# Rows of cumulated logs made in place by TensorE for ten chunks, and four units' low words shifted by ScalarE

## The chip, the cores and the metric

The kernel runs on one core of a Trainium2 chip. The metric is the device time of one execution in microseconds (us). Five engines work side by side, each through its own queue in order: TensorE (PE, with its weight loads shown apart as PEld), VectorE (DVE), ScalarE (ACT), GpSimd (POOL) and SyncE (SP), which here only issues transfers.

## The reference

A state-space layer in chunks, then a two-matrix layer with an activation of its own. In the reference:

```python
log_a = np.log(np.clip(a, 1e-06, 1.0))
for c in range(nc):
    cum = np.cumsum(la, axis=-1)
    L = np.exp(cum[:, :, :, None] - cum[:, :, None, :]) * causal
    M = np.einsum('bhin,bhjn->bhij', Cc, Bc) * L
    y[:, :, sl] = M @ xc + (C @ state) * exp(cum)
    state = exp(sum(la)) * state + sum_j B x exp(cum_last - cum)
h = y_as_rows @ w_in          # 3072 x 256 by 256 x 2048
out = (h - np.tanh(h)) @ w_out
```

The batch is 4, there are 8 heads of dimension 32, the state has 16 entries, the sequence 768 steps. `moe_w_in` and `moe_w_out` arrive as 64-bit floats.

## The kernel before

**Tiling.** A sequence is cut into chunks of 112 steps (the last has 96); the 28 chunks of the four batches are numbered so that chunk `ck` is step block `ck // 4` of batch `ck % 4`. The first 16 of the 128 partitions carry the state, so that one matmul does the state's part and the chunk's own. The second layer works on column tiles of the 3072 tokens: four of 256 (`t` = 0 to 3), then four of 512. The first tile needs the outputs of chunks 0, 1 and 2; its hidden units are taken in eight "units" `u` of 256. In a first sweep the four small tiles use units 0 and 1 alone, later sweeps take the small tiles in pairs.

**Order.** Nothing is issued directly. Each step is announced with `op(engine, cost, function, reads, writes)` to a planner (`Order`, L64). It knows the dependences and a cost for each step, plans by a list schedule in several rounds with random jitter (from `SEED`), takes the best plan, and issues the functions in its order of start times. Tags such as `po0` or `ph` stand for places in PSUM or SBUF with a number of buffers; a new holder waits for the readers of the old one. `urge` moves a step ahead.

**Decay factors.** The exponent of chunk, head, i, j is `cum_i - cum_j`. The kernel has three ways:
- Chunks 0 to 3 (`first_tile`, L435): for each half of the heads POOL cuts the logs to a triangle (`fn_k`, L443), PE adds a mask of -32768 (`fn_f`, L448) and sums the triangle with four full f32 matmuls (L451), ACT takes the exp (`fn_x`, L467), PE makes the products of B and C (`fn_p`, L461), DVE multiplies (`fn_m`, L471). The mask is in the exponent, so nothing is cut afterwards.
- Chunks 4 to 9 (`chunk_a`, L494): the row sums are split by DVE into three bf16 parts (`split`, L1039), stored to memory (`put_parts`, L1050) and read back in eight small transfers (`get_parts`, L1053) into `lt_c` and `rt_c`, beside rows of ones (`ones`, L989) and signs (`signs`, L993). Four bf16 matmuls of nine rows (L507) then give the exponents next to the products (L512) in one PSUM tile `att`; ACT exp (L516), DVE product (L520), and POOL cuts the upper triangle (`cut`, L532).
- Chunks 10 on (`chunk_l`, L535): rows of sums are broadcast from memory (`cumr`), ACT subtracts through its bias (L550), POOL cuts.

`chunk_y` (L623) multiplies the factors with x (L637); its tag is `po0` for odd chunks under 4, else `po1`. `prep` (L378) fills the state's rows and the decayed B on POOL; `state` (L562) starts the running state.

**Weights.** `conv(u)` (L314) turns a unit's 64-bit words into f32 and then into a high and a low part: ACT scales the high words (`fn0`, L325), DVE shifts the low words by 29 (`fn1`, L330), clamps (L335) and puts the bits together (L338, L345), ACT rounds to the high part (L349), DVE subtracts (L352). Units 0 and 1 come in halves. The first tile multiplies units 0 and 1 in plain f32 (`plain`, L756), and the small tiles take their second matrix as f32 too (L834); all else uses three products of high and low parts (`mm1` L763, `mm2` L844), with tanh (L794), difference (L798), and the split of the result (L802, L808) between them.

Of the kernel before, what the change touches and what calls it, by code (L numbers as in the profile page):

```python
# [222 lines left out]
def tile_ssm_moe(ctx: ExitStack, tc: tile.TileContext, a, x, bn, bc, wts, out):  # L223
# [90 lines left out]
    def conv(u, halves=False):  # L314
# [12 lines left out]
        def fn1(s):  # L327
            if s.start == 0:
                wm[u] = p1.tile([P, 2, 512], U32, tag="wm", name=f"wm{u}")
            nc.vector.tensor_scalar(out=wm[u][:, s], in0=raws[u][:, s, :, 0], scalar1=29, scalar2=None,  # L330
                                    op0=ALU.logical_shift_right)
# [103 lines left out]
    def first_tile():  # L435


        n_a = op.pieces(slot("att", 1), 2)
        place = {}

        def fn_k(ck, i):
            chs[ck]["k", i] = p3.tile([P, BANK], F32, tag="g", name=f"lm{ck}_{i}").rearrange("p (h m) -> p h m", h=4)
            nc.gpsimd.affine_select(out=chs[ck]["k", i], in_=la[:, 4 * i : 4 * i + 4, ck : ck + 1].broadcast_to([P, 4, P]),  # L443
                                    pattern=[[0, 4], [-1, P]], compare_op=ALU.is_gt, fill=0.0, base=0, channel_multiplier=1)

        def fn_f(ck, i):
            f = chs[ck]["f", i] = ps_h.tile([P, 4, P], F32, tag="ph", name=f"cp{ck}_{i}")
            nc.tensor.matmul(out=f[:, :, 0:Q], lhsT=eye, rhs=never.unsqueeze(1).broadcast_to([P, 4, Q]),  # L448
                             start=True, stop=False, skip_group_check=True)
            for h in range(4):  # L450
                nc.tensor.matmul(out=f[:, h, 0:Q], lhsT=chs[ck]["k", i][:, h], rhs=upto[:, N:P], start=False, stop=h == 3,  # L451
                                 skip_group_check=True)

        def fn_p(ck):
            if ck == 0:
                att = ps_a.tile([P, 4, 4 * P], F32, tag="att", name="att0")
                place[0] = att[:, :, 0 : 4 * Q].rearrange("p i (k q) -> p i k q", k=4)
            bb, cc = operands(ck)
            for i in range(4):
                r = slice(32 * i, 32 * i + 2 * N)  # L460
                nc.tensor.matmul(out=place[0][:, i, 2 * (ck % 2) : 2 * (ck % 2) + 2], lhsT=bb[r], rhs=cc[r],  # L461
                                 start=True, stop=True)
# [11 lines left out]
        for ck in range(FIRST):
            urge = URGE if ck < len(chunks[0]) else 0.0
            k = chs[ck]
            k["n_l"] = op.pieces(slot("lt", NL), 2)
            if ck % CPG == 0:
                prep(ck // CPG)
            for i in range(2):  # L480
                n_f, n_k = slot("ph", NPH), slot("g", 3)
                op("POOL", 0.7, lambda ck=ck, i=i: fn_k(ck, i), r=["la"], w=[n_k], urge=urge)
                op("PE", 1.14, lambda ck=ck, i=i: fn_f(ck, i), r=[n_k, "upto", "never"], w=[n_f])
                op("ACT", 0.52, lambda ck=ck, i=i: fn_x(ck, i), r=[n_f, "tab"], w=[k["n_l"][i]], urge=urge)
                if i == 0:
                    op("PE", 0.59, lambda ck=ck: fn_p(ck), r=[grp[ck // CPG]["n_bc"]], w=[n_a[ck % 2]])
                op("DVE", 0.6, lambda ck=ck, i=i: fn_m(ck, i), r=[n_a[ck % 2]], w=[k["n_l"][i]], urge=urge)
            if ck == 0:
                for i in range(4):
                    for j in range(2):  # L490
                        op("SP", 0.7, lambda i=i, j=j: get_parts(i, j), r=["cum3"], w=[("lt_c", "rt_c")[j]], dma=KB // 2)
            chunk_y(ck)

    def chunk_a(ck):  # L494

        d, k, q = grp[ck // CPG], chs[ck], qlen(ck)
# [1 line left out]
        n_a = slot("att", 1)  # L500

        def fn_p():
# [7 lines left out]
            for i in range(4):  # L510
                r = slice(32 * i, 32 * i + 2 * N)
                nc.tensor.matmul(out=at_[:, i, 2:4, :], lhsT=bb[r], rhs=cc[r, :, 0:q], start=True, stop=True)  # L512
# [687 lines left out]
```

## Time and profile before

| what | us |
|---|---|
| median of three runs | 324.19 |
| lowest and highest | 323.92, 324.3 |
| the profiled execution's own time | 324.25 |
| its span, first to last instruction | 322.6 |
| PE busy in the span | 313.7 |
| DVE, ACT, POOL busy | 215.3, 210.3, 60.6 |

The profile is a record of one execution. Times of the timeline count from the start of the span. A line of a timeline has start, duration, engine, line of the kernel, operation, the written and read tiles, the shape and the number of instructions; in brackets stands how long the engine was idle before it and what it waited for. "SPq" rows are the issue of a transfer, not the transfer. Matmuls overlap: the distance between the starts of two says what one costs, the duration also holds its latency. An f32 matmul leaves two records.

### The profile page before, as it was taken

What the parts mean: (1) busy time and instruction counts of PE and PEld (TensorE: products, weight loads), DVE (VectorE), ACT (ScalarE), POOL (GpSimd) and SP (SyncE); (2) the same over time, 40 slices, a digit from 0 to 9 for tenths busy, and PEclk for the clock granted to TensorE, in tenths of its full rate; (3) what the DMA queues carried; (4) which work ended last, traced back from release to release, by engine and by line L of the source; (5) the groups of instructions that cost most, each with busy time, mean ns of one, the idle gap of its engine ahead of it and who ended that gap; (6) DMA issues with size and microseconds to landing.
All of it is one profiled execution on the core that took longest, in us unless ns stands there. A gap on an engine that the chain in (4) does not pass through costs nothing.

```text
span 322.6 us, 5757 instructions
## 1 busy us (share of the span) xinstructions
PE 313.7 (97%) x2160; PEld 255.3 (79%) x2160; DVE 215.3 (67%) x314; ACT 210.3 (65%) x471; POOL 60.6 (19%) x94
## 2 busy tenths in 40 slices
PE   8997999999999999999999999999999999999995
PEld 7765888788888878787878887888878788888883
DVE  6978997898888867457563864664765645645552
ACT  6568888477687888575945854966868544534451
POOL 8604424003122514402300400111102000000000
PEclk9999999999999999999999999999999999999999
DMA  6679557539433149280606005005420000100001
GB/s 205 195 238 325 173 162 307 183 94 346 89 65 66 30 98 272 48 241 5 205 0 207 16 0 209 1 2 226 168 61 0 2 0 0 68 1 0 2 0 65
DMA packets 15451, 35.27 MB, mean 109 GB/s; under 512 B 2464, under 2 KB 4416, under 8 KB 15424
## 3 DMA queue, kind: packets, MB, share of 16 engines
q1 hardware_dynamic: 13696, 31.76, 29.4%
q0 software_dynamic: 1728, 3.15, 5.7%
q8 instruction: 17, 0.28, 0.4%
q14 instruction: 10, 0.08, 0.1%
HBM read 28.32 MB, written 3.43 MB: 98 GB/s over the span
## 4 chain that ended last, share of the span: by engine, by line
PE 91%; DVE 5%; ACT 2%; issue 1%
PE ph L763 39%; PE o L844 38%; PE o L834 3%; PE y L704 3%; PE att L678 3%; PE y L637 1%; PE warm L1003 1%; DVE lt L471 1%; ACT lt L550 1%; DVE lt L520 1%; DVE wv L345 1%; PE att L461 1%; PE cp L451 1%; ACT lt L516 1%; DVE wm L338 1%
## 5 line engine op out<-in xcount | busy, mean ns | idle before, releaser
L798 DVE TENSOR_TENSOR g<-ph,g 128x512 f32<-128x512 f32 x96 | 65.7, 688 | 52.1 <-ACT g L794 52.0
L794 ACT ACTIVATE g<-ph 128x512 f32<-128x512 f32 x96 | 57.3, 598 | 48.7 <-PE ph L763 47.8
L808 DVE TENSOR_TENSOR gl<-g,gh 128x512 fp32r<-128x512 f32 x88 | 62.7, 715 | 31.0 <-ACT gh L802 29.5
L763 PE MATMUL ph<-xh,wh 128*128 128x512 f32 (+1 forms) x200 | 76.0, 382 | 0.0
L763 PE MATMUL ph<-xh,wl 128*128 128x512 f32 (+1 forms) x200 | 74.8, 377 | 0.0
L802 ACT CAST gh<-g 128x512 fp32r<-128x512 f32 x88 | 54.4, 620 | 28.3 <-DVE g L798 26.4
L844 PE MATMUL o<-gh,wh 128*128 128x512 f32 x176 | 69.2, 393 | 0.0
L844 PE MATMUL o<-gl,wh 128*128 128x512 f32 x176 | 68.5, 389 | 0.0
L844 PE MATMUL o<-gh,wl 128*128 128x512 f32 x176 | 68.5, 389 | 0.0
L763 PE MATMUL ph<-xl,wh 128*128 128x512 f32 (+1 forms) x200 | 59.0, 376 | 0.0
L532 POOL TENSOR_SCALAR_AFFINE_SELECT lt<-lt 128x896 f32<-128x896 f32 (+1 forms) x24 | 23.3, 969 | 128.4 <-ACT lt L550 118.3
L763 PEld LDWEIGHTS ph<-xh,wh 128*128 128x128 f32 x200 | 37.6, 188 | 7.6 <-issue 0.6
L763 PEld LDWEIGHTS ph<-xh,wl 128*128 128x128 f32 x200 | 37.6, 188 | 6.8
L763 PEld LDWEIGHTS ph<-xl,wh 128*128 128x128 f32 x200 | 36.7, 188 | 7.0
L550 ACT ACTIVATE lt<-lt,ncum 128x112 f32<-128x112 f32 (+1 forms) x144 | 41.7, 375 | 0.0
L844 PEld LDWEIGHTS o<-gh,wh 128*128 128x128 f32 x176 | 33.0, 188 | 7.8 <-issue 0.8
L844 PEld LDWEIGHTS o<-gl,wh 128*128 128x128 f32 x176 | 33.0, 188 | 6.9
L844 PEld LDWEIGHTS o<-gh,wl 128*128 128x128 f32 x176 | 33.1, 188 | 6.7
L684 DVE TENSOR_TENSOR lt<-att,lt 128x896 f32<-128x896 f32 (+1 forms) x18 | 18.9, 1052 | 0.0
L888 POOL DMA_DIRECT2D pt<-part x12 | 11.1, 1023 | 41.1 <-ACT part L885 38.1
L834 PE MATMUL o<-g,wf 128*128 128x256 f32 x64 | 15.4, 384 | 1.4 <-ACT x L578 0.9
L605 ACT CAST xh<-y 128x224 fp32r<-128x224 f32 (+4 forms) x18 | 7.3, 413 | 13.1 <-DVE s L711 10.6
(97 smaller groups left out, 275.0 us busy)
## 6 DMA issues: line engine op xcount, KB each, us to landing
lt<-cumr SPq DMA_DIRECT2D x18, 512.0 KB
raw<-w_d SPq DMA_DIRECT2D x16, 512.0 KB
bc<-bc_d SPq DMA_DIRECT2D x14, 352.0 KB
x<-x_d SPq DMA_DIRECT2D x14, 256.0 KB
pt<-part POOLq DMA_DIRECT2D x12, 256.0 KB, 4.5
out_d<-ob SPq DMA_DIRECT2D x8, 256.0 KB
braw<-bn_d SPq DMA_DIRECT2D x14, 112.0 KB
out_d<-pt SPq DMA_DIRECT2D x4, 256.0 KB
```

Of the source, the lines that this page charges most:

```text
L532: nc.gpsimd.affine_select(out=k["l"][:, :, 0:q], in_=k["l"][:, :, 0:q], pattern=[[0, H], [1, q]], compare_op=ALU.is_ge, fill=0.0, base=N, ...
L550: nc.scalar.activation(k["l"][:, h, 0:q], k["l"][:, h, 0:q], AF.Exp, bias=ncum[:, h, ck : ck + 1])
L678: nc.tensor.matmul(out=a_[:, i], lhsT=bb[r], rhs=cc[r, :, 0 : qlen(ck)], start=True, stop=True)
L684: nc.vector.tensor_tensor(out=l, in0=chs[j]["a"], in1=l, op=ALU.mult)
L763: nc.tensor.matmul(out=ph[:, i * w : i * w + w], lhsT=w_[:, u, 0, k, j * P : (j + 1) * P], rhs=(xh, xl)[p][:, k, ts], start=p == 0 and k = ...
L794: nc.scalar.activation(g[:, 0:used], gs[t, f][0][:, 0:used], AF.Tanh)
L798: nc.vector.tensor_tensor(out=g, in0=ph, in1=g, op=ALU.subtract)
L802: nc.scalar.copy(gh[:, 0:used], gs[t, f][1][:, 0:used])
L808: nc.vector.tensor_tensor(out=gl[:, 0:used], in0=g[:, 0:used], in1=gh[:, 0:used].bitcast(F32), op=ALU.subtract)
L834: nc.tensor.matmul(out=po[t, seg][e], lhsT=wf[:, u, 256 * j + e * P : 256 * j + (e + 1) * P], rhs=gs[t, f][1][:, i * w : i * w + w], start ...
L844: nc.tensor.matmul(out=po[t, seg][e], lhsT=w_[:, u, 1, j, e * P : (e + 1) * P], rhs=g[:, i * w : i * w + w], start=f == seg[0] and k == 0 ...
L888: op("POOL", 1.0, lambda e=e: nc.gpsimd.dma_start(out=pts[m][:, e], in_=obs[t, e], accum_op=ALU.add), r=[name, n_pt[2 * m], n_pt[2 * m + 1 ...
```

## The change

- `first_tile` with its POOL triangles, PE masks and full f32 sums is gone, and so are `masks`, `ones`, `signs`, the bf16 parts, `put_parts` and `get_parts`.
- A second log `twin` holds each log of chunks 0 to 9 four times. `rows_of(g)` (chunks 0 to 3, 4 to 7, 8 and 9) multiplies slices of it with the triangle of ones: each gives rows of cumulated logs, several copies of each, at the partitions where they are needed. For g = 0 they are used in f32 straight from PSUM; for g = 1 and 2 ACT rounds a copy to fp32r and DVE adds the rest into other rows. ACT and DVE then make `lt_c[g]` and `rt_c[g]` by a scale and a bias per partition (`sel`, made by `sels`).
- Chunks 0 to 9 all go through the new `chunk_a`. Exponents (`exps`) and products have a half each of one PSUM tile (`room`) that stays; the exponents of chunk `ck + 1` are issued beside the products of chunk `ck`. Chunks 0 to 2 are announced in the start, chunk 3 in the loop with the others. All ten are cut by POOL.
- The low words of units 0 to 3 (`EASED`) are shifted by an ACT copy with a scale of 2^-29 and a rounding bias in place of DVE's shift.
- The column sums move from the tile `pr` to `po0`; the rows tile goes to the tag `pt`. `SEED` is 152 for 266.

```diff
-FIRST = 4
+EASED = 0, 1, 2, 3
...
+            if u in EASED:
+                nc.scalar.activation(wm[u][:, s], raws[u][:, s, :, 0], AF.Copy, scale=2.0 ** -29, bias=-0.5 - 2.0 ** -20)
+                return
...
-            op("DVE", 0.7 * k, lambda s=s: fn1(s), r=n_r, w=[n_m[i]])
+            op(*(("ACT", 1.02 * k) if u in EASED else ("DVE", 0.7 * k)), lambda s=s: fn1(s), r=n_r, w=[n_m[i]])
...
+    def room(i):
+
+        if "room" not in misc:
+            misc["room"] = ps_a.tile([P, 4, 4 * P], F32, tag="att", name="att0")
+            misc["att"] = op.pieces(slot("att", 1), 2)
+        return misc["room"][:, :, 0 : 4 * Q].rearrange("p i (k q) -> p i k q", k=4)[:, :, 2 * i : 2 * i + 2]
+
+    def rows_of(g):
+
+        cks = range(4 * g, min(4 * g + 4, JOINT))
+        tag = "ph" if g < 2 else "po0"
+        n_p = slot(tag, NPH if g < 2 else 1)
+
+        def fn():
+            pk = misc["pk", g] = (ps_h if g < 2 else ps_o).tile([P, 4, P], F32, tag=tag, name=f"rows{g}")
+            for c, ck in enumerate(cks):
+                for i in range(4):
+                    nc.tensor.matmul(out=pk[32 * i : 32 * i + 32, c], rhs=upto, start=True, stop=True,
+                                     lhsT=twin[:, 4 * H * ck + 8 * i : 4 * H * ck + 8 * i + 32])
...
+        op("PE", 0.1 + 0.85 * k, fn, r=["twin", "upto"], w=[n_p])
+        n_s = n_p
+        if g:
+            n_s = slot("g", 3)
+            op("ACT", 0.2 + 0.42 * k, fn_h, r=[n_p], w=[n_s])
+            op("DVE", 0.15 + 0.57 * k, fn_y, r=[n_p, "sel"], w=[n_s])
+        op("ACT", 0.2 + 0.42 * k, fn_l, r=[n_s, "sel"], w=[f"lt_c{g}"])
+        for w in range(2):
+            op("DVE", 0.15 + 0.47 * k, lambda w=w: fn_r(w), r=[n_s, "sel"], w=[f"rt_c{g}.{w}"])
+
+    def exps(ck, early):
+
+        k, g, ex = chs[ck], ck // 4, room(0)
+        k["n_l"] = [slot("lt", NL)]
+
+        def fn():
+            for i in range(4):
+                r = slice(32 * i, 32 * i + 8)
+                nc.tensor.matmul(out=ex[:, i], lhsT=lt_c[g][r, ck - 4 * g], rhs=rt_c[g][r, :, ck - 4 * g], start=True, stop=True)
...
+        if ck == 0:
+            fn, r, then = exps(0, True)
+            op("PE", 0.55, fn, r=r, w=[n_e], urge=urge)
+            then()
+        fn_e, r_e, then = exps(ck + 1, early) if ck + 1 < JOINT else (None, [], lambda: None)
+        if early:
+            op("PE", 0.6, fn_p, r=[d["n_bc"]], w=[n_b], urge=urge)
+            op("PE", 0.55, fn_e, r=r_e, w=[n_e], urge=urge)
+        elif fn_e:
+            op("PE", 0.7, lambda: (fn_p(), fn_e()), r=[*r_e, d["n_bc"]], w=[n_e, n_b])
+        else:
+            op("PE", 0.6, fn_p, r=[d["n_bc"]], w=[n_b])
+        then()
+        op("DVE", 1.08, fn_m, r=[n_b], w=k["n_l"], urge=urge)
+        op("POOL", 1.1, lambda: cut(ck), w=k["n_l"], urge=urge)
...
-        tag = "po0" if ck % 2 and ck < FIRST else "po1"
+        tag = "po0" if ck % 2 and ck < NB else "po1"
...
+    twin = p2.tile([P, 4 * H * JOINT + 32], F32, tag="wv", name="twin")
...
+    def twins():
+        nc.scalar.activation(twin[:, 0 : 4 * H * JOINT].rearrange("p (c h d) -> p c h d", h=H, d=4),
+                             a_sb.rearrange("p c b h -> p (c b) h")[:, 0:JOINT].unsqueeze(3).broadcast_to([P, JOINT, H, 4]), AF.Ln)
...
+    lt_c = [cp.tile([P, min(4, JOINT - 4 * g), P], F32R if g else F32, name=f"lt_c{g}") for g in range(3)]
+    rt_c = [p2.tile([P, 2, 4, Q], F32R if g else F32, tag="ob", name=f"rt_c{g}") for g in range(2)]
+    rt_c.append(cp.tile([P, 2, JOINT - 8, Q], F32R, name="rt_c2"))
...
+    rows_of(0)
     n_pr = slot("po1", 1)
     op("PE", 0.95, sums_rows, r=["la", "upto"], w=[n_pr])
...
+    rows_of(1)
+    rows_of(2)
+    n_pq = slot("po0", 1)
+    op("PE", 0.55, lambda: sums_cols(upto, "pq"), r=["la", "upto"], w=[n_pq])
...
-    first_tile()
-    for G in range(-(-FIRST // CPG), 2):
+    for G in range(2):
         prep(G)
+    for ck in chunks[0]:
+        chunk_a(ck, True)
+        chunk_y(ck)
     conv(0, True)
```

More of the change, by code (lines that the diff above doesn't have):

```diff
@@ L433, in operands @@
         return bb, cc
[L435 to L457, printed above, removed]
@@ new lines, in exps, with fn_x @@
+    def exps(ck, early):
[5 more added lines that the diff above has]
+                nc.tensor.matmul(out=ex[:, i], lhsT=lt_c[g][r, ck - 4 * g], rhs=rt_c[g][r, :, ck - 4 * g], start=True, stop=True)
+        def fn_x():
+            k["l"] = p3.tile([P, H, P], F32, tag="lt", name=f"lt{ck}", bufs=NL)[:, :, N:P]
+            nc.scalar.activation(k["l"].rearrange("p (i w) q -> p i w q", i=4), ex, AF.Exp)
+        return fn, [f"lt_c{g}", f"rt_c{g}.0", f"rt_c{g}.1"], lambda: op("ACT", 0.92, fn_x, r=[misc["att"][0], "tab"], w=k["n_l"],
+                                                                     urge=URGE if early else 0.0)
@@ L458, in fn_p, with chunk_a @@
+    def chunk_a(ck, early=False):
+        d, k, pr_ = grp[ck // CPG], chs[ck], room(1)
+        n_e, n_b = misc["att"]
+        urge = URGE if early else 0.0
+        def fn_p():
             bb, cc = operands(ck)
@@ L474, in first_tile @@
[L474 to L492, printed above, removed]
@@ L658, in chunk_y @@
         else:
-            op("PE", cost, fn, r=r, w=w)
+            op("PE", cost, fn, r=r, w=w, urge=URGE if ck < len(chunks[0]) else 0.0)
         moved = []
@@ L987, in stay @@
                                   in_=idn[0:N].unsqueeze(1).broadcast_to([N, CPG * H, N]))
-    def ones():
-        v = lt_c.rearrange("p c m -> p (c m)")
-        nc.scalar.copy(v, nc.const_aps.tensor(1.0, (P, 1), F32).broadcast_to(v.shape))
-    def signs(w):
-        v = rt_c[:, w].rearrange("p c q -> p (c q)")
-        nc.vector.tensor_scalar(out=v, in0=nc.const_aps.tensor(1.0, (P, 1), F32).broadcast_to(v.shape),
-                                scalar1=par[:, w : w + 1], scalar2=None, op0=ALU.mult)
     def warm():
@@ L1007, in tile_ssm_moe @@
     op("POOL", 1.6, consts_pool, w=["upto", "after", "pid"])
-    op("POOL", 1.0, masks, w=["never"])
     op("DVE", 0.25, logs, r=["al"], w=["a"])
+    op("ACT", 0.46, twins, r=["al", "a", "tab"], w=["twin"])
     op("ACT", 0.4, lambda: nc.scalar.activation(la.rearrange("p h (c b) -> p c b h", b=NB), a_sb, AF.Ln), r=["a", "tab"], w=["la"])
-    op("DVE", 1.2, consts_dve, r=["pid"], w=["idn", "par"])
+    op("DVE", 1.2, consts_dve, r=["pid"], w=["idn"])
+    op("DVE", 0.9, sels, r=["idn"], w=["sel"])
     op("ACT", 1.4, lambda: table(1), r=["la"], w=["tab"])
     op("POOL", 1.2, stay, r=["idn"], w=["bi"])
-    op("ACT", 0.9, ones, w=["lt_c"])
-    for w in range(2):
-        op("DVE", 0.85, lambda w=w: signs(w), r=["par"], w=["rt_c"])
     for G in range(2):
@@ L1068, in tile_ssm_moe @@
-    op("DVE", 0.36, lambda: split(0), r=[n_pr], w=["rows"])
-    op("DVE", 1.4, lambda: [split(i) for i in range(1, 6) if i != 4], r=["rows"], w=["parts"])
-    for i in range(2):
-        op("SP", 0.42, lambda i=i: put_parts(i), r=["parts"], w=["cum3"], dma=KB)
+    op("DVE", 0.36, lambda: nc.vector.tensor_copy(out=rows[0:HR], in_=misc["pr"][0:HR, 0:2]), r=[n_pr], w=["rows"])
     for i in range(2):
         op("SP", 0.42, lambda i=i: put_rows(i), r=["rows"], w=["cumr"], dma=KB // 2)
+    rows_of(1)
```

127 lines of the change are left out of this document (41 added, 86 removed).

## The prediction

> **What bounds the kernel now.** The page's first part and clock row were read first, then busy time by stages cut where TensorE (PE) changes its state.
>
> ```profile
> span 322.6 us, 5757 instructions
> ...
> PEclk9999999999999999999999999999999999999999
> ```
>
> ```profile
> core 0: us, PE busy (x) PEld busy (x) DVE busy (x) ACT busy (x) POOL busy (x), PEclk, DMA share, GB/s
> ...
> 4.37:21.16 16.79, 15.76 (x189) 12.99 (x188) 13.75 (x25) 8.70 (x18) 9.40 (x15) 1.00 0.70 213
> 21.16:36.00 14.84, 12.16 (x208) 9.41 (x205) 13.10 (x18) 12.75 (x30) 4.98 (x7) 1.00 0.91 302
> 36.00:57.21 21.21, 20.71 (x267) 17.38 (x265) 18.67 (x25) 17.48 (x49) 7.15 (x9) 1.00 0.57 205
> ...
> 64.00:313.30 249.30, 249.30 (x1398) 203.30 (x1397) 159.72 (x228) 163.60 (x364) 35.66 (x47) 1.00 0.28 82
> ```
>
> The first number is the stage, the second its length, the third PE's busy time. From 64 us to 313.3 PE is busy 249.30 of 249.30 us at full clock; nothing that the change touches is issued there. So the end moves by as much as PE's state at about 60 us moves. That has two parts: when PE starts on the first tile's weights (21.16 us, the L756 row below), and what PE does and loses after that. From 21.16 to 57.21 (36.05 us) PE is busy 12.16 + 20.71 = 32.87 us and idle 3.2.
>
> Before 21.16 PE is also busy, but with the logs: the chain of work that ended last runs there over matmuls that the change takes away.
>
> ```profile
> 16.82 0.88 PE cp L451 x8
> 17.69 0.59 PE att L461 x8
> 18.28 0.95 PE y L637 x32
> ...
> 19.65 0.97 PE y L637 x32
> ```
>
> So the question is how early the chain that replaces this can reach the first-tile matmul, and what it leaves behind.
>
> **The change part by part.** These timeline rows carry the durations (start, duration, engine, line).
>
> ```profile
> 0.85 3.59 PE L1003 MATMUL warm<-const-float32-1.0 128*32 128x128 f32 x16 [0.85 <-PEq L1187]
> ...
> 3.13 0.28 DVE L968 TENSOR_SCALAR a_sb<-a_sb 128x224 f32<-128x224 f32 x1 [0.91 <-DMA a_sb<-a_d]
> ...
> 3.44 0.61 ACT L1010 ACTIVATE la<-a_sb 128x224 f32<-128x224 f32 x1 [0.41 <-DVE a_sb L968]
> 4.06 1.28 ACT L981 ACT_TABLE_LOAD   x1
> ...
> 4.37 1.06 PE L1032 MATMUL pr<-upto,la 128*112 128x128 f32 x4
> ...
> 5.85 0.42 DVE L1042 COPY both<-pr 112x256 f32<-112x256 f32 x1 [0.69 <-PE pr L1037]
> ...
> 8.36 0.68 ACT L325 ACTIVATE wv<-raw 128x512 f32<-128x512 f32 x1 [0.90 <-DMA raw<-w_d]
> 8.36 1.04 PE L451 MATMUL cp<-upto,lm 128*128 128x112 f32 x8
> ...
> 14.79 0.66 PE L461 MATMUL att<-bc 32*128 32x224 f32 x8
> ...
> 18.21 0.97 PE L637 MATMUL y<-lt,x 128*32 128x112 f32 x32
> ...
> 21.16 1.99 PE L756 MATMUL ph<-xf,wv 128*128 128x256 f32 x8
> 21.31 0.92 ACT L516 ACTIVATE lt<-att 128x896 f32<-128x896 f32 x1 [0.26 <-PE att L512]
> 22.26 1.09 DVE L520 TENSOR_TENSOR lt<-att,lt 128x896 f32<-128x896 f32 x1 [0.79 <-ACT lt L516]
> ...
> 24.77 0.98 POOL L532 TENSOR_SCALAR_AFFINE_SELECT lt<-lt 128x896 f32<-128x896 f32 x1
> 24.78 1.51 DVE L345 SCALAR_TENSOR_TENSOR wv<-wv,wm 128x512 uint32<-128x512 uint32 x1
> ```
>
> And these groups of instructions (busy, mean ns, up to 66 us) the prices.
>
> ```profile
> L443 POOL TENSOR_SCALAR_AFFINE_SELECT lm<-la 128x512 f32<-128x512 f32 x8 | 6.7, 843 | 1.0 <-PE cp L451 0.9
> ...
> L798 DVE TENSOR_TENSOR g<-ph,g 128x512 f32<-128x512 f32 x9 | 6.1, 681 | 1.1 <-ACT g L794 1.1
> ...
> L325 ACT ACTIVATE wv<-raw 128x1024 f32<-128x1024 f32 x3 | 3.5, 1166 | 0.0
> ...
> L330 DVE TENSOR_SCALAR wm<-raw 128x1024 uint32<-128x1024 uint32 x3 | 2.9, 954 | 0.1
> ...
> L330 DVE TENSOR_SCALAR wm<-raw 128x512 uint32<-128x512 uint32 x4 | 2.2, 556 | 0.0
> ...
> L601 ACT COPY xf<-y 128x224 f32<-128x224 f32 x3 | 1.0, 346 | 1.3 <-PE y L637 1.3
> ```
>
> *The new start chain.* The clamp L968 ends at 3.41. The log is now taken first of 320 elements (ten chunks, eight heads, four copies): 0.61 at 224 elements, and from L601 (224 in 0.346) to L516 (896 in 0.92) an element costs 0.00085 us, so 0.7, to 4.15. PE followed the log by 0.32 us (4.05 to 4.37): 4.45. rows_of(0) is 16 f32 matmuls of 128 columns in four column groups. Nearest is L637: 16 of 112 columns (two records each) in the same four groups, 0.97; so 1.1, to 5.55. If the groups did not overlap at all, each would cost what the two warm-up records did, at most 3.59 / 8 = 0.45 us (L1003), 7.2 together; that far end I keep as a bound only, since L637 has the very shape. Two VectorE (DVE) multiplies from PSUM then make rt_c0: L1042 takes 0.42 for 256 elements, L798 0.68 for 512, so 0.6 each for 448, 1.2 with the hand-over to 7.0. ScalarE (ACT) loads its second table meanwhile (1.28) and makes lt_c0 (about 0.6). exps of chunk 0: four f32 matmuls of 224 columns in row groups, as L461, 0.66: 7.75.
>
> From here the three first chunks form a loop: exp 0.92 (L516) empties the one place for exponents, PE refills it in 0.66, with hand-overs of 0.1 each 1.75 us a chunk. exp of chunk 2 ends at 7.8 + 2 x 1.75 + 0.92 = 12.2. Then product 1.09 (L520), the mask on GpSimd (POOL) 0.98 (L532, on this path now for chunks 0 to 2), y about half of 0.97, copy 0.35 (L601), hand-overs 0.2: 15.3. In the loop's gaps (0.8 us a round on ACT, 0.7 on DVE) unit 0's first half must pass: it lands at 8.36, and needs 0.68 for L325, as much for the low words, and three DVE instructions of 0.4 to 0.7. I add one ACT and one DVE instruction in the way, 1.3: first tile at **16.6**. Bounds: nothing in the way, 15.3; all of the conversion in the way (1.4 on ACT, 1.8 on DVE) and a stretched DVE instruction, 18.9. Such stretching shows at 24.78: L345 takes 1.51 beside the mask at 24.77. Eight L443 (6.7 us of POOL) go and four masks (3.9) come, so I count no more of it in all. A result of zero gain would need the chain to reach 19.7 or later.
>
> *Queues.* SP no longer issues ten small transfers of log parts.
>
> ```profile
> 11.38 0.87 SPq L1056 DMA_DIRECT2D lt_c<-cum  x1
> ...
> 15.98 0.43 SPq L1058 DMA_DIRECT2D rt_c<-cum  x1
> ...
> 17.35 0.42 SPq L296 DMA_DIRECT2D raw<-w_d  x1
> ```
>
> Eight of them fill SP from 11.38 to 16.41, ahead of unit 1's first half (17.35), on which the second first-tile matmul depends. These 5.0 us go, about as much as the first tile moves (4.6), so the loads keep their distance to it; I count nothing for them. If they did not move, unit 1 would be late by up to those 4.6 and the gain of the start would go. The two put_rows stay.
>
> *DVE and ACT.* DVE loses the parts (5.85 to 8.83 less the kept 0.42, 2.5 us), the signs (1.85), and L330 of four units: 4 x 0.556 and, for the two whole ones, 2 x 0.954, 4.1 in all; the new selectors, row sums and multiplies add about 4.5. Net -4. It was busy 31.8 of the 36.05 us after the first tile, so it gets no worse. ACT gains the low words: 4 x 0.68 + 2 x 1.17 = 5.1 us; that an ACT copy of integers costs what L325 does (same source, stride and size) is the assumption, from below 0.6 (L330's rate) to 1.4 (twice). Of it 3.7 us (units 1 to 3) fall behind the first tile, and with chunk 3's exp 4.6; ACT is idle 36.05 - 12.75 - 17.48 = 5.8 us there. So it is covered, by 1.2 us. The row-sum copies of chunks 4 to 9 (about 2 us on ACT) fall into the start, where ACT is busy 8.70 of 16.79.
>
> *Moved behind the first tile.* Chunk 3 was done at the start; now its products (0.6), its y (0.45) and f32 exponents (0.5) come after it, on PE: **+1.5**. Chunks 4 to 9 kept their products; their exponents go from bf16 to fp32r.
>
> ```profile
> 23.45 0.28 PE L507 MATMUL att<-rt_c,lt_c 9*128 9x224 bf16 x4
> ...
> 23.55 0.57 PE L512 MATMUL att<-bc 32*128 32x224 f32 x8
> ```
>
> The next matmul starts 0.10 after L507: that is its price in bf16. At fp32r it is not shown at 224 columns; between 0.10 and the f32 price of about 0.5, six times: 0 to +2.4. I take 0, as the records of L763's fp32r matmuls come one for a matmul, like bf16, where f32 has two.
>
> **The sum**, on the profiled execution (span 322.6, its time 324.25; median of the runs 324.19, the same within 0.06): first tile 21.16 to 16.6, -4.6; chunk 3, +1.5; PE's 3.2 us of idle after the first tile unchanged, 0. Together -3.1: **321.1 us**. Idle may fall by up to 1.5, since DVE has 4 us less to do.
>
> **The clock.** The list of PE's waits from 21 to 64 us begins with its longest:
>
> ```profile
> PE o L834 <- ACT x L578: 0.9, 1, 0.9
> ```
>
> PEclk is 9 in all slices and 1.00 in all stages; still the warm-up matmuls (L1003) took 0.45 us for 128 columns where L451 takes 1.04 / 4 = 0.26 for 112, or 0.30 for 128: PE starts 1.5 times slower, for 3.6 us. The new start has PE working some 10 of 12 us, in pieces; a gap long enough to bring the slow start back would cost 3.6 x (1 - 1/1.5) = 1.2. [...] The warm-up rows agree with a slow start, though no row of the granted clock shows one.
>
> **The rivals.**
> - *The start does not shorten enough.* Chunk 1's y needs PSUM po0, now freed only after rows_of(2), its copy, its sum, the column sums and the decay weights: six hops over PE, ACT and DVE. Free of queues they take about 4 us and are done near 10, with room to spare before chunk 1's mask (12.5). It decides from there: with two instructions of 0.9 us ahead of each of its four ACT and DVE hops it ends at 17.2, and two y and a copy later the first tile stands at 18.8; with one mask beside a DVE instruction (+0.8) at 19.5. Against: its instructions are ready early and short. 324.25 - 1.66 + 1.5 = 324.1.
> - *ACT becomes the bound (slower).* After the first tile 4.6 us come to 5.8 us of idle; much of that idle is waits for PE in short pieces. If none fits, all 4.6 delay tanh and with it PE: 324.25 - 4.6 + 1.5 + 4.6 = 325.75. It is slower from where over 3.1 of the 4.6 is not hidden. For it: 12.75 of 14.84 busy at 21 to 36; against: 17.48 of 21.21 at 36 to 57.
> - *fp32r exponents cost as f32:* +2.4, 323.5.
> - *A gap of PE in the start brings its slow state back:* +1.2, 322.4.
> - *The idle goes too:* -1.5 and the chain at 15.3: 318.3 to 319.5.
>
> **How the numbers follow.** Forecast 0.57 (319.6 to 322.6), start too long 0.10, ACT 0.12, fp32r 0.08, clock 0.06, idle gone 0.07. The range 318.9 to 324.4 leaves out ACT's case and the tails of the first and last rival, under 0.2. About 0.2% (0.65 us) is what can be told from no change: faster (under 323.5) 0.57 + 0.07 + 0.06 + half of 0.08 = 0.74; same 0.11 (the other half and most of the first rival); slower 0.15 (ACT, and the rest of the first).
>
> **What would show it.** The first L756-kind matmul near 16.6; three 0.9 us exps 1.75 apart from about 7.8; no parts transfers, unit 1's load issued near 12; PE idle about 3 us between it and the end of the fourth small tile; PE full after that, the rest shifted by 3. Wrong: tanh waiting behind low-word copies, the mask on POOL behind a load, or PE below 1.00.

## The result and the profile after

| | before | after |
|---|---|---|
| median of four runs each (us) | 324.06 | 329.50 |
| lowest and highest | 323.48, 324.30 | 329.33, 329.91 |
| span of the profiled execution | 322.6 | 327.6 |
| first-tile matmul starts | 21.16 | 24.87 |

The ratio is 1.0173, with a 95% interval of 1.0155 to 1.019. The change makes the kernel slower, where faster was forecast, and the time lies outside the forecast's range.

The page's first line and its clock row, and busy time by stages:

```profile
span 327.6 us, 5837 instructions
...
PEclk9657999999999999999999999999999999999999
```

```profile
core 0: us, PE busy (x) PEld busy (x) DVE busy (x) ACT busy (x) POOL busy (x), PEclk, DMA share, GB/s
4.12:24.87 20.75, 16.16 (x270) 10.43 (x269) 13.99 (x25) 13.66 (x26) 7.55 (x10) 0.66 0.70 233
24.87:36.00 11.13, 10.69 (x119) 7.93 (x116) 9.55 (x13) 8.38 (x21) 5.07 (x5) 0.87 0.71 221
36.00:64.00 28.00, 26.57 (x360) 22.30 (x364) 21.76 (x27) 23.55 (x60) 10.88 (x11) 1.00 0.48 155
64.00:318.50 254.50, 254.50 (x1434) 207.67 (x1427) 165.45 (x235) 165.67 (x368) 35.96 (x47) 1.00 0.29 89
```

From 64 us on PE is full again (254.50 of 254.50 at 1.00), so the loss was made earlier. Up to the first tile the granted clock, which stood at 1.00 in every stage of before, averages 0.66.

The timeline of PE in the start:

```profile
4.12 2.39 PE L454 MATMUL rows<-upto,twin 128*32 128x128 f32 x80
...
7.65 0.66 PE L495 MATMUL att<-rt_c,lt_c 8*128 8x224 f32 x8 [0.52 <-DVE rt_c L473]
8.13 0.56 PE L516 MATMUL att<-bc 32*128 32x224 f32 x8
8.70 0.65 PE L1041 MATMUL pq<-la,upto 128*128 128x224 f32 x2
11.08 1.13 PE L495 MATMUL att<-rt_c,lt_c 8*128 8x224 f32 x8 [1.74 <-DVE lt L520]
13.25 1.13 PE L516 MATMUL att<-bc 32*128 32x224 f32 x8 [1.04 <-ACT lt L499]
...
15.66 1.13 PE L495 MATMUL att<-rt_c,lt_c 8*128 8x224 f32 x8 [0.24 <-DVE lt L520]
...
24.87 3.45 PE L767 MATMUL ph<-xf,wv 128*128 128x256 f32 x8
...
29.47 1.99 PE L767 MATMUL ph<-xf,wv 128*128 128x256 f32 x8
```

The same four exponent matmuls take 0.66 at 7.65 and 1.13 at 11.08; the first tile's matmul takes 3.45 where the second, of the same shape, takes 1.99. Between lies half clock (0.50 in the windows below). The brackets show the second thing: L495 waits for DVE's product (L520), and L516 for ACT's exp (L499), though exponents and products have a half each of the tile `att`. ACT and DVE show the same turns:

```profile
9.01 0.90 ACT L499 ACTIVATE lt<-att 128x896 f32<-128x896 f32 x1
...
12.28 0.92 ACT L499 ACTIVATE lt<-att 128x896 f32<-128x896 f32 x1 [1.27 <-PE att L495]
...
16.86 0.92 ACT L499 ACTIVATE lt<-att 128x896 f32<-128x896 f32 x1 [2.56 <-PE att L495]
```

```profile
14.51 1.09 DVE L520 TENSOR_TENSOR lt<-att,lt 128x896 f32<-128x896 f32 x1 [2.59 <-PE att L516]
...
19.84 1.09 DVE L520 TENSOR_TENSOR lt<-att,lt 128x896 f32<-128x896 f32 x1 [2.54 <-PE att L495]
```

At 19.84 DVE multiplies chunk 2, and what ended its wait were L495's matmuls, the exponents of chunk 3, which go to the other half. Chunk 2's own products had been done at 18.95 (17.82 and 1.13), so only the last 0.9 of the 2.54 is owed to them. So exponents (1.13), exp (0.92), products (1.13) and multiplication (1.09) run one behind the other; with hand-overs that is 4.58 us from 11.08 to 15.66.

Short windows show when the clock falls and returns:

```profile
9.00:10.00 1.00, 0.34 (x2) 0.00 (x0) 0.80 (x3) 1.00 (x3) 0.00 (x0) 1.00 1.03 395
10.00:10.50 0.50, 0.00 (x0) 0.00 (x0) 0.50 (x1) 0.50 (x2) 0.00 (x0) 1.00 1.15 386
10.50:11.00 0.50, 0.00 (x0) 0.00 (x0) 0.50 (x2) 0.50 (x1) 0.00 (x0) 0.79 1.04 305
11.00:12.00 1.00, 0.92 (x8) 0.52 (x8) 0.92 (x3) 0.01 (x1) 0.70 (x2) 0.50 1.02 349
...
27.50:28.00 0.50, 0.50 (x3) 0.33 (x2) 0.50 (x1) 0.00 (x0) 0.47 (x1) 0.65 0.90 360
28.00:29.00 1.00, 1.00 (x18) 0.56 (x20) 0.96 (x2) 0.00 (x0) 0.00 (x0) 1.00 0.09 33
```

It falls at about 10.8, inside the wait before 11.08, and returns some 3 us after the first tile's matmul began: about 17 us at 0.50.

### The profile page after: what moved, and what is told of

It is laid out like the page before. It is cut to its first block, busy times and chain, and to the rows that moved or that the text cites. A ratio compares the mean times of both kernels' runs of the same rounds, so it can differ in the third digit from the quotient of the medians.

```text
span 327.6 us, 5837 instructions
## 1 busy us (share of the span) xinstructions
PE 316.3 (97%) x2200; PEld 255.0 (78%) x2200; DVE 214.8 (66%) x315; ACT 215.0 (66%) x478; POOL 61.9 (19%) x87
## 4 chain that ended last, share of the span: by engine, by line
PE 88%; DVE 4%; ACT 3%; issue 3%; POOL 1%; ACTq 0%; DVEq 0%; POOLq 0%
PE ph L774 38%; PE o L855 37%; PE o L845 3%; PE y L715 3%; PE att L689 3%; DVE lt L520 2%; ACT lt L499 2%; PE warm L1010 1%; PE att L516 1%; PE att L495 1%; POOL lt L543 1%; PE y L648 1%; ACT lt_c L470 0%; DVE rt_c L473 0%; DVE wv L337 0%
## 5 line engine op out<-in xcount | busy, mean ns | idle before, releaser
L805 ACT ACTIVATE g<-ph 128x512 f32<-128x512 f32 x96 | 57.1, 596 | 51.3 <-PE ph L774 51.1
L543 POOL TENSOR_SCALAR_AFFINE_SELECT lt<-lt 128x896 f32<-128x896 f32 (+1 forms) x28 | 30.6, 1092 | 141.8 <-ACT lt L561 122.1
L520 DVE TENSOR_TENSOR lt<-att,lt 128x896 f32<-128x896 f32 x10 | 10.9, 1086 | 7.2 <-PE att L516 2.6
```

Source lines behind the costliest of these rows:

```text
L520: nc.vector.tensor_tensor(out=lt, in0=pr_, in1=lt, op=ALU.mult)
L543: nc.gpsimd.affine_select(out=k["l"][:, :, 0:q], in_=k["l"][:, :, 0:q], pattern=[[0, H], [1, q]], compare_op=ALU.is_ge, fill=0.0, base=N, ...
L805: nc.scalar.activation(g[:, 0:used], gs[t, f][0][:, 0:used], AF.Tanh)
```

## The experiments

The theories: **clock** (half clock costs), **turns** (one PSUM tile makes the chain serial), **ACT** (the forecast's slower rival: the low words burden ScalarE), **order** (the planner's order is bad), **parts** (which of the change's parts costs). Ratios are against the kernel before, run beside each experiment (323.76 to 324.16 us). "Fill" is a matmul of ones into a place that nobody reads; it adds work and changes no value. "Planned anew" means that the planner found another order for the edited kernel; e1 and e9 keep the changed kernel's order, e8 and e12 that of e7, e18 that of e17.

### The clock alone

The changed kernel in its own order, with fills of 512 columns behind four exponents and three products (e1), or four lighter ones in `exps` and `sums_cols` (e9, the diff).

```diff
+            if ck in (1, 2):
+                fill(512 if ck == 1 else 256)
...
+        fill(512 if k == "pq" else 256)
```

> The changed kernel in its own order of instructions, plus seven f32 matmuls of ones (512 columns, about 0.85 us each at full clock, results unused) on TensorE, one behind each of the first four exponent steps and the first three product steps. Theory clock: the 5.4 us come mostly from the granted clock of 0.5 between 10.8 and 27.9 us, since TensorE has too little to do in the start; with the fill the clock stays at 1.00, each chunk loses two steps at half speed (about 1.0 us a chunk) and the first-tile matmul costs 1.7 in place of 3.45: about 324.5, first tile near 21.5. Theory banks: the halves of the exponent and product tile lie in the same four PSUM banks and are worked in turn, 4.6 us a chunk; the clock is a side effect: 328 or more, the fill only in the way.

Measured: 329.36 us, 1.0194 (1.0156 to 1.0233), clock 1.00, first tile 24.60.

> The changed kernel with four more matmuls of ones and no other edit: 512 columns behind the exponents of chunk 1 and behind the log transposes of the products' first part, 256 behind the exponents of chunk 2 and behind the transposes of its second part. It keeps PE from long stretches of sparse work without one extra matmul in every step. Theory A (the half clock by itself costs: the first tile's matmul ran 3.45 us for 1.99, the sparse matmuls 1.13 for 0.66): the granted clock is 0.99 or more, the first tile starts by 23.5 and takes 2.0, and the time is 326.0 to 328.0, since about 1.5 us of the first tile and 1 to 2 us of the chain go. Theory B (the chain is set by the turns that exponents and products take in one tile, and PE's own rate in it matters little): the clock may rise, but the first tile stays at 24 or later and the time is 328.3 to 329.6. If the clock stays at half from about 11 us on, the run tells neither.

Measured: 326.99 us, 1.0100 (1.0082 to 1.0118). PE in e9:

```profile
8.59 0.66 PE L502 MATMUL att<-rt_c,lt_c 8*128 8x224 f32 x8 [0.55 <-DVE rt_c L473]
...
12.02 0.66 PE L502 MATMUL att<-rt_c,lt_c 8*128 8x224 f32 x8 [0.88 <-DVE lt L529]
...
15.66 0.66 PE L502 MATMUL att<-rt_c,lt_c 8*128 8x224 f32 x8 [0.28 <-DVE lt L529]
...
22.48 1.99 PE L776 MATMUL ph<-xf,wv 128*128 128x256 f32 x8
```

```profile
8.00:12.00 4.00, 2.59 (x21) 1.37 (x20) 3.80 (x8) 3.80 (x7) 0.44 (x1) 1.00 1.04 373
12.00:16.00 4.00, 3.70 (x30) 1.91 (x30) 3.05 (x4) 2.03 (x3) 1.30 (x2) 1.00 0.96 298
```

The first tile comes 2.4 us sooner and its matmul takes 1.99; the time falls by 2.5 us, and the two intervals don't touch. The planned order is the same and nothing but the fills differs, so this is the clock's part, with what the fills cost already taken off. In e1 the clock was full as well and nothing was won: there the fills stood in the chain themselves, seven of them at 1.06 each (8.31 to the next start at 9.37). The exponents still start 3.43 and 3.64 us apart: turns are left.

### Turns

e4: for chunks 0 to 2 exponents in two banks, products in the other two, heads in two halves, one tile as before.

```diff
+        def place(i, w):
+            if early:
+                return misc["room"][:, 2 * w + i % 2, 0 : 2 * Q].rearrange("p (k q) -> p k q", k=2)
```

> The changed kernel with exponents and products of chunks 0 to 2 in banks of their own (two banks each, taken in two halves of the heads), chunks 3 to 9 with exponents and products in one step (planned anew). Theory banks: the loop takes 2.3 to 2.8 us a chunk in place of 4.6, the first tile comes 3 to 5 us sooner, 324.5 to 326.5 even if the clock falls. Theory clock alone: TensorE is still thinly used, the clock still falls, 328 or more.

Measured: 337.54 us, 1.0442 (1.0415 to 1.0469), clock 0.968, first tile 32.34. Own banks did not part the two: the exponents of a chunk's second half still waited 0.90 for DVE's product of the first (11.21 us). That wait went by the tile and not by the bank, and twice as many steps took turns. The kernel was also planned anew.

e5: the planner is told that the halves are one place.

```diff
-            misc["att"] = op.pieces(slot("att", 1), 2)
+            misc["att"] = [slot("att", 1)] * 2
```

> The changed kernel, one line: the planner gets one name for both halves of the exponent and product tile, so that it plans with the waits that the chip's trace shows between them. Nothing else is changed (planned anew). Theory order (new): the halves wait for each other on the chip but not in the plan, VectorE's queue stands behind products that come late (5 us idle between 12 and 20 us), and the conversions of units 0 and 1 behind them start late: told of it, the plan puts conversions ahead, 325 to 327.5, VectorE idle under 3 us from 12 to 20. Theory serial loop: the turn-taking itself (3.7 us a chunk) is the cost, whatever the order: 329 to 330.

Measured: 331.6 us, 1.0233 (1.0214 to 1.0251), clock 0.974, first tile 27.01.

e6: e5, and exponents and products of a chunk in one step.

```diff
-            op("PE", 0.6, fn_p, r=[d["n_bc"]], w=[n_b], urge=urge)
-            op("PE", 0.55, fn_e, r=r_e, w=[n_e], urge=urge)
...
+            op("PE", 0.7, lambda: (fn_e(0), fn_p(0)), r=[*r_e, d["n_bc"]], w=[n_e, n_b])
```

> The changed kernel with exponents and products of a chunk in one step on TensorE, then exp, then product, as the kernel before had it for chunks 4 to 9; the planner knows it. Theory order: 325 to 327.5. Theory serial loop: 329 or more, with 3.4 to 3.9 us a chunk in the start.

Measured: 328.77 us, 1.0147 (1.0127 to 1.0167), clock 0.978, first tile 23.84. A planner that knows of the turns finds no order that wins more than 0.7 us; the turns stay.

e7: two tiles of two banks, heads 0 to 3 and 4 to 7, each with its own exponents and products. e8: e7 with a fill of 512 columns behind each half step of chunks 0 to 2. e12: the same with 128, and 256 behind the column sums.

```diff
-            misc["room"] = ps_a.tile([P, 4, 4 * P], F32, tag="att", name="att0")
+            misc["room"] = [ps_a.tile([P, 2, 4 * P], F32, tag="att", name=f"att0_{e}") for e in range(2)]
...
+            if early:
+                fill(P)
```

> The changed kernel with the PSUM place cut into two tiles of two banks, one for heads 0 to 3 and one for heads 4 to 7; each half does exponents and products in one step, exp, product, and does not wait for the other; the planner knows it. Two exps of 0.54 and two products of 0.62 a chunk in place of one of 0.92 and one of 1.09; chunks 10 on have two products each too. Theory serial loop: with two halves in flight the loop takes 2.3 to 2.8 us a chunk, first tile near 20, 323 to 326. Theory order alone: as the joint kernel, within 1 us. Theory clock: TensorE stays thin, the clock falls and the gain is given back: 327 or more with a granted clock under 1.

Measured: 328.88 us (326.93 to 331.51), 1.0179 (1.0109 to 1.0249), clock 0.976, first tile 22.58 and 3.78 long. With two tiles the first tile comes 2.3 us sooner than in the changed kernel, at half clock as there; the order is another one. The four runs are two pairs: 326.93 and 326.97 at a mean clock of 0.976 to 0.977, 330.78 and 331.51 at 0.962 to 0.963. The same program in the same order is some 4 us slower where the half clock lasts longer. PE in e7, by the windows:

```profile
8.00:12.00 4.00, 2.67 (x29) 1.89 (x30) 3.93 (x9) 3.86 (x8) 0.46 (x2) 1.00 1.02 364
12.00:16.00 4.00, 4.00 (x46) 2.64 (x40) 4.00 (x7) 2.88 (x7) 2.32 (x3) 0.61 1.06 338
16.00:20.00 4.00, 3.63 (x40) 2.29 (x32) 3.00 (x5) 2.70 (x6) 2.56 (x4) 0.50 0.85 303
```

By the 0.61 from 12 to 16 us the clock falls at about 12.9, and between 8.62 and there no wait of PE was longer than 0.44. From 12 to 16 PE is busy without a break, after the fall mostly with matmuls of 8 or 32 rows or 32 columns, and the clock still stands at 0.50 from 16 to 20.

> The two-tile kernel with an f32 matmul of ones (0.85 us) behind each half step of chunks 0 to 2 on TensorE. If the clock falls in the two-tile kernel and costs time, this one keeps 1.00 and is 1 to 3 us faster; if the clock costs nothing because other engines set the pace, it is equal or slower.

Measured: 328.26 us, 1.0134 (1.0117 to 1.0152), clock 1.00, first tile 25.46.

> The changed kernel with two PSUM tiles of two banks for exponents and products (heads 0 to 3 and 4 to 7), so that one half's exp and product run beside the other half's matmuls, and a matmul of ones of 128 columns behind each half step of chunks 0 to 2, 256 behind the two parts of the log transposes. With 512 columns in each place the same form took 328.26 at full clock, with none 328.88 at 0.976. Theory A (clock and turn-taking are the two parts of the loss, and the full fill stood in the path): the clock is 0.99 or more, the first tile starts by 22.5 and takes 2.0, 325.5 to 327.5. Theory B (something else in the start sets the first tile, such as the conversion of unit 0 or GpSimd's masks): first tile at 24 or later and 328 or more. If the clock falls to half again, only the fill's size is told.

Measured: 325.69 us, 1.0054 (1.0035 to 1.0074), clock 0.999. PE in e12, by the windows:

```profile
8.00:12.00 4.00, 3.56 (x24) 2.56 (x24) 3.44 (x7) 3.27 (x8) 0.21 (x1) 1.00 1.04 391
12.00:16.00 4.00, 4.00 (x41) 2.90 (x40) 3.31 (x7) 2.19 (x4) 1.38 (x2) 1.00 0.86 270
16.00:20.00 4.00, 4.00 (x52) 2.94 (x48) 2.85 (x5) 3.06 (x8) 2.18 (x4) 1.00 0.85 280
```

Here PE no longer waits for ACT or DVE: from 12 to 20 us it is full. But what fills it are the fills, and halves that cost as much each as whole groups did: two exponents take 0.48 to the next start, as four did in the changed kernel (7.65 to 8.13).

```profile
8.44 0.65 PE L508 MATMUL att<-rt_c,lt_c 8*128 8x224 f32 x4 [0.55 <-DVE rt_c L472]
8.92 0.55 PE L511 MATMUL att<-bc 32*128 32x224 f32 x4
```

Against e7, in the same order, the light fills win 1.3 us over its faster pair of runs and 5.5 over the slower. It is the fastest version with the new start, and still slower than before.

### Halves after the start, and the order

Two tiles in the start only, whole chunks afterwards (e13, SEED 253); e12 in another order (e14, SEED 15); the changed kernel in another order (e16, SEED 266).

```diff
+            op("PE", 1.0 if g == 0 else 0.7, fn_all, r=[f"lt_c{g}", f"rt_c{g}.0", f"rt_c{g}.1", d["n_bc"]], w=misc["att"])
```

> The two-tile form with its 128-column matmuls of ones (325.69 us), with chunks 3 to 9 issued whole again: one step of PE writes both tiles, four exponents and four products, where a half took 0.21 + 0.48 us by its own, so 1.38 for a chunk where a whole one takes 0.70. SEED is 253, of 300 seeds the one with the shortest plan. If the rest of the loss lies in what the halves cost PE after the first tile (seven chunks by up to 0.68, less those that the planner already put side by side), the time is 322.5 to 324.8 and the form is even with the kernel before or below it; if the loss lies in the start before the first tile, 325.0 to 326.5.

Measured: 327.18 us, 1.0098 (1.0064 to 1.0132).

> The two-tile form with its 128-column matmuls of ones and no other edit than SEED 15 for 152, of 300 seeds the one with the shortest plan (1.34 us below that of 152). If the planner's plan says something of the chip, 324 to 325.5 against 325.69; if the order is noise to the chip, anything within 1.5 us of 325.69. It says how far the first-tile time of this form hangs on the order.

Measured: 327.3 us, 1.0101 (1.0069 to 1.0134). Both have the first tile early enough, 22.06 and 22.20, and lose behind it; e14's PE:

```profile
22.20 1.99 PE L760 MATMUL ph<-xf,wv 128*128 128x256 f32 x8 [0.59 <-ACT xf L604]
27.86 1.99 PE L760 MATMUL ph<-xf,wv 128*128 128x256 f32 x8 [2.47 <-DVE wv L347]
```

Unit 1's conversion on DVE is late by 2.47 us, where e12's second matmul had waited 0.34. So the order alone moves this form by 1.6 us, the shorter plan was the slower kernel, and e13 does not say what the halves cost.

> The changed kernel at SEED 266, the one of the kernel before, in place of 152; its plan is 1.6 us longer. If the loss of 5.4 us is an accident of one order, another order moves it by several us, to below 327 or above 332; if it lies in the steps themselves, the time stays between 328 and 332 and TensorE's granted clock falls to half in the start again.

Measured: 328.51 us, 1.0140 (1.0102 to 1.0177), clock 0.979, first tile 26.04. Another order is worth about 1 us and the loss stays, with its half clock. Two of its runs stand at 327.44 and 327.93 with a mean clock of 0.979, two at 329.1 and 329.3 with 0.973 to 0.974, as in e7. The seed alone moved these two forms by 1 to 1.6 us, and the hybrid below by 4.0 (e10 and e15): forms that differ in order can be compared to no better than that.

### The parts

The low words back to DVE (e2), and alone in the kernel before (e3).

```diff
-EASED = 0, 1, 2, 3
+EASED = ()
```

> The changed kernel without the low words on ScalarE (EASED empty, VectorE shifts them all; planned anew). Theory ScalarE: its 5 us of copies hold up the start and the first sweep: 326 or less. Theories clock and banks: the copies are not the cause, the clock still falls: 328.5 to 331.

Measured: 332.53 us, 1.0274 (1.0256 to 1.0292), first tile 26.08.

> The kernel before with the low words of units 0 to 3 on ScalarE and nothing else (planned anew). Theory ScalarE: 326 or more. Otherwise VectorE's relief is worth little or something: 323 to 324.3, clock 1.00.

Measured: 324.38 us, 1.0020 (1.0005 to 1.0035). Without ScalarE's copies the changed kernel is 3 us slower, not faster, and by themselves they change nothing. Since e2 was planned anew, what they are worth within the change is not shown. The theory of ACT as the bound falls.

The kernel before with chunks 4 to 9 from rows in place and chunks 0 to 3 as they were: e10, and e15 in a better planned order (SEED 199).

```diff
-    op("DVE", 1.4, lambda: [split(i) for i in range(1, 6) if i != 4], r=["rows"], w=["parts"])
+    rows_of(1)
+    rows_of(2)
...
-        op("PE", 0.65, fn_p, r=[d["n_bc"], "lt_c", "rt_c"], w=[n_a])
+        op("PE", 0.65, fn_p, r=[d["n_bc"], f"lt_c{ck // 4}", f"rt_c{ck // 4}.0", f"rt_c{ck // 4}.1"], w=[n_a])
```

> The kernel before, with the start of chunks 0 to 3 as it was (bf16 parts of chunks 4 to 9 and their transfers leave; no low words on ScalarE), and chunks 4 to 9 from rows made in place by rows_of(1) and rows_of(2), with fp32r exponents. Theory A (the loss comes from the start of chunks 0 to 3): the first tile stays between 20 and 22.5 and the time is 323.5 to 325.5. Theory B (the rows made in place or the fp32r exponents of chunks 4 to 9 cost by themselves): the exponents' steps behind the first tile take 0.38 each where they took 0.10, which is 6 x 0.28 = 1.7 us, and the two sets of rows 2.4 us of PE each; 326 to 329.

Measured: 330.73 us, 1.0214 (1.0195 to 1.0233). The first tile stood at 25.38, both its matmuls side by side: the order had moved, and the run says nothing of the part. It differs from e15 by the seed alone.

> The kernel before with chunks 4 to 9 from rows made in place and chunks 0 to 3 as they were, now at SEED 199 (of 300 seeds the shortest plan, 3.5 us shorter than that of the first try, which put the first tile's two matmuls side by side at 25.38). Theory A (the loss comes from the new start of chunks 0 to 3): the first tile stays between 20 and 22.5 and the time is 323.0 to 325.5. Theory B (rows in place for chunks 4 to 9 cost by themselves, their copies and sums standing before the first tile on ScalarE and VectorE): 326 or more, or a first tile after 23.

Measured: 326.76 us, 1.0110 (1.0060 to 1.0160), clock 1.00, first tile 23.86. ACT in e15:

```profile
20.10 0.66 ACT L325 ACTIVATE wv<-raw 128x512 f32<-128x512 f32 x1 [1.98 <-POOL bw L388]
20.67 0.57 ACT L505 CAST high<-rows 128x512 fp32r<-128x512 f32 x1
21.14 0.60 ACT L640 COPY xf<-y 128x224 f32<-128x224 f32 x2
21.61 0.40 ACT L505 CAST high<-rows 128x256 fp32r<-128x256 f32 x1
22.06 0.81 ACT L516 ACTIVATE lt_c<-high,sel 128x512 fp32r<-128x512 f32 x1
```

The copies (L505) and the scaling (L516) of the rows stand among the first tile's own copies (L640). The longest delay there is the 1.98 us before 20.10. The profile names POOL, but `twin` has one of the two buffers of `wv`, and in this order PE reads it until 19.90 (the `rows` matmuls, L500, start at 17.62 and 19.28); so unit 1's conversion (L325) probably waits for `twin`, and the copies of y, which was ready at 19.46, stand behind it. The changed kernel has its `rows` done by 6.51. With bf16 parts DVE split the rows early and transfers put them in place. So both orders tried of this part lose, 7.0 and 2.6 us; that it must lose, or that it loses so within the change, is not shown.

The complement: chunks 0 to 3 by `rows_of(0)`, chunks 4 to 9 by bf16 parts, low words on DVE (e17, SEED 196), and the same order with e9's four fills (e18).

```diff
+    rows_of()
     n_pr = slot("po1", 1)
...
-                op("PE", 1.14, lambda ck=ck, i=i: fn_f(ck, i), r=[n_k, "upto", "never"], w=[n_f])
...
+            op("PE", 0.6, fn, r=misc["rows"], w=[n_e], urge=urge)
+            op("ACT", 0.92, fn_x, r=[n_e, "tab"], w=k["n_l"], urge=urge)
```

> The complement of the hybrid: chunks 0 to 3 through rows_of(0), f32 exponents and POOL's cut as in the change, all four in the start; chunks 4 to 9 by bf16 parts through memory as before; low words on VectorE as before. SEED 196, of 300 seeds the shortest plan (0.3 us longer than that of the kernel before). Theory A (the loss lies in the new start itself, half clock and turns in one tile): the granted clock falls to half between 10 and 25 us, the first tile starts after 23 and takes over 3, and the time is 326 to 330. Theory B (the start alone is sound, and what breaks it are the rows of chunks 4 to 9, whose matmuls, copies and sums stand before the first tile): first tile by 20.5 and 320.5 to 324.

Measured: 332.5 us, 1.0255 (1.0217 to 1.0293), clock 0.968. Its exponents are eight matmuls of 112 columns a chunk where the changed kernel has four of 224. PE in e17:

```profile
8.80 0.57 PE L504 MATMUL att<-bc 32*128 32x224 f32 x8
12.65 1.11 PE L488 MATMUL att<-rt_c,lt_c 8*128 8x112 f32 x16 [3.28 <-DVE lt L508]
...
18.97 1.13 PE L504 MATMUL att<-bc 32*128 32x224 f32 x8 [1.33 <-ACT lt L492]
...
25.65 3.78 PE L792 MATMUL ph<-xf,wv 128*128 128x256 f32 x8 [0.47 <-ACT xf L637]
```

> The same kernel in the same order, with four matmuls of ones, 512 columns behind the exponents of chunk 1 and the first column sums, 256 behind the exponents of chunk 2 and the second column sums. If half clock is a part of what the new start loses, the clock is 0.99 or more, the first tile's matmul takes 2.0 and the time falls by 1.5 to 3 us against the run without them, as it did in the changed kernel (329.5 to 326.99). If the clock of the run without them stays at full, this run is slower by the 1.6 us or less that the matmuls of ones take.

Measured: 332.49 us, 1.0282 (1.0258 to 1.0305), clock 0.972. The new start alone brings the turns, the half clock and the late first tile. In e18 the first two fills came before the long wait (3.17 us, up to 12.29) and the clock fell all the same, so e18 does not part the clock from the rest. The parts do not add up: +8.7 us (e17) and +2.6 (e15) against +5.4 for the whole, which has the copies on ScalarE and another order. Each is one order.

## Why the prediction was wrong

**What bounds the kernel** held: PE is full from 64 us on and the end moved with PE's state. The span grew by 5.0; the first tile came 3.71 later, and what lies behind it gave 1.3 more, where +1.5 was forecast. The whole error lies in the first tile: 16.6 forecast, 24.87 measured, 8.3 us.

**The step that failed is the loop of 1.75 us a chunk** in the new start chain, with the clock beside it. Its parts:

- *Up to exp of chunk 0*, forecast at 7.8, measured 9.01: 1.2. The exponents' matmuls were near, 7.65 for 7.0: DVE and ACT took turns on the tile of the first rows (`rt_c`, `lt_c`, `rt_c` at 5.26, 6.04, 6.85, the last after a wait of 0.85 for ACT), then ACT had the other rows' copies ahead of the exp.
- *The loop*, exp 0 to exp 2, forecast 3.5 for two rounds, measured 7.85: 4.4. The forecast let PE refill the exponents as soon as exp had emptied them. The two halves are columns of the same four banks of one tile, and each step waited for the other half's reader (1.74 us at 11.08, 1.04 at 13.25). So a round is the sum of exponents, exp, products and multiplication, and not exp and refill alone (whose own terms, by the way, add up to 1.78). At full clock (e9) the two rounds take 6.44 (9.95 to 16.39), fills included; the other 1.4 belong to the clock. Own banks in one tile did not free them in e4 (a wait of 0.90); why the halves wait for each other, no run shows.
- *From exp 2 to the first tile*, forecast 4.4, measured 7.1 (17.78 to 24.87): 2.7. The multiplication of chunk 2 began 2.06 after the exp had ended, behind its products at half clock and chunk 3's exponents; y took 0.97 where half was counted. The last copy was done at 23.55 and the weights at 16.20 (L347), but PE had products of chunk 3, exponents of chunk 4 and a state step ahead of the first tile until 24.87.

**The clock** was a rival with 0.06 and a price of 1.2. It decided more: e9 puts it at 2.5 at least. The forecast looked for one long gap; that a gap brings the slow matmuls of the warm-up back was its estimate, and no run shows it. The wait before 11.08 had lasted 1.2 to 1.7 us when the clock fell; the 4 us around it held 2.26 us of PE work. In e9, with 2.59 of the same 4 us busy and waits of 0.55 and 0.88, it stayed at 1.00. Neither the longest wait nor the busy share tells it, though: in e7 it fell at about 12.9 with PE busy 2.67 of the 4 us up to 12, and all the time from there, and no wait over 0.44 after 8.62; in e15, whose mean over the whole span is 1.00, it did not fall from 20 to 24 us, with PE busy 1.83 of 4 and a wait of 1.64 (to 21.54). In e17 it fell at about 12.8 (0.91 from 12 to 13), right behind a wait of 3.28. What decides it, the shapes of the matmuls or something else, stays open.

**The other steps.** *Queues*: right at nothing; the second first-tile matmul followed the first by 4.60 us (before 5.28). *DVE and ACT*: right that ACT covers the low words (e3); the ACT rival falls. *Chunk 3 behind the first tile*: forecast +1.5, total behind the first tile +1.3, but by other terms, so that the two lie close is luck. Of chunk 3 only y came behind it (28.95); its exponents (18.73) and products (23.06) stood ahead of it. The first tile's matmul itself took 1.46 more (3.45 for 1.99), and idle behind it fell from the forecast's 3.2 to 1.87 (24.87 to 64 us), about as the rival "the idle goes too" had it. *fp32r exponents*, taken at nothing. PE's timeline before and after:

```profile
32.55 0.58 PE L512 MATMUL att<-bc 32*128 32x224 f32 x8
33.06 0.59 PE L637 MATMUL y<-lt,x 128*32 128x112 f32 x16
```

```profile
38.68 0.66 PE L516 MATMUL att<-bc 32*128 32x224 f32 x8
39.00 0.44 PE L495 MATMUL att<-rt_c,lt_c 8*128 8x224 f32 x4
39.38 0.39 PE L774 MATMUL ph<-xh,wh 128*128 128x256 f32 x1
```

A step of products and exponents takes 0.70 here and took 0.61 before (its exponents began 0.10 ahead of L512, at 32.45), so 0.09 each, some 0.5 us for six: near the cheap end of the bounds.

*The sum*: −4.6 became +3.7, +1.5 became +1.3. The rival of a start that is too long had the right place and too small a price. It named `po0`, which was freed late indeed, at 18.36 (the decay weights, L1060 at 18.00) where near 10 was counted; but PE had products and exponents to do until chunk 1's y at 19.63, and no wait is put down to it. Its first tile came at 18.8, or 19.5 with a mask in the way. The upper end of the rival "the idle goes too" adds up to 319.6, not 319.5, which changes nothing.

**What stays open.** At full clock with light fills the new start reaches the first tile between 22.06 (e13) and 22.74 (e12), and with heavy ones at 24.60 (e1) and 25.46 (e8); all are behind the 21.16 of before, whether by turns, halves or fills. So of the 5.4 us the clock's 2.5 is shown by runs. The turns are shown as waits in the traces, but what they cost in time apart from the order is not. A form without turns that doesn't double the steps wasn't tried; nor was a start whose clock holds without fills. No version that was run beats the kernel before.

## What to carry to other kernels

A chain through several engines is counted by places, not by engines: here two halves of one PSUM tile were one place (waits of 1.74, 1.04 and, in e4, 0.90 us), and a round of the loop over them cost the sum of its four steps (1.13, 0.92, 1.13 and 1.09, with hand-overs 4.58 us), not the longest pair. Work that is removed from TensorE in a stretch where it waits for others may have been what kept its clock up (up to the first tile it was busy 15.76 of 16.79 us at 1.00 before, 16.16 of 20.75 at 0.66 after); look at the granted clock of the new stretch before anything else, since neither its longest gap nor its busy share foretold it here. And a replacement that is shorter on one engine but stands in the chain (rows, copies, scalings) can lose to a longer one that runs beside it (transfers, masks). Where a planner sets the order, one seed of each form compares little: here a seed was worth up to 4 us.

## What the runs showed of the hardware

- The granted clock fell to 0.50 within a wait of 1.74 us, in a stretch where small matmuls kept TensorE busy 2.26 of 4 us, and came back only some 3 us into the first tile's matmuls, 17 us later (0.79 from 10.5 to 11 us, 0.65 from 27.5 to 28). In e7 3.1 us of full work did not bring it back: from its fall at about 12.9 to 16 us PE was busy without a break, mostly with matmuls of 8 or 32 rows or 32 columns, and from 16 to 20 us the clock was 0.50 with PE busy 3.63 of 4.
- How long the half clock lasted is an estimate from the windows' mean clocks, taken as 1.00 or 0.50 throughout: 17.1 us in the changed kernel (10.79 to 27.85) and in e17 (12.82 to 29.88, from 0.91 from 12 to 13 and 0.56 from 29 to 30), 20.5 in e4 (13.6 to 34.1, from 0.70 from 12 to 16 and 0.66 from 30 to 36).
- At the start the same 80 records of `rows` took 2.39 us in the changed kernel (from 4.12) and 3.25 in e9 (from 4.17), with the granted clock shown as 1.00 in both; what cost 0.9 us more in the one does not show in that column.
- ScalarE's scale and bias from two columns of SBUF took 0.78 us for 512 elements out of PSUM (`lt_c`, L470 at 6.04), where the forecast had 0.6; tanh out of PSUM takes 0.596 for as many (L805).
